# The opening of a Fourier mixing and SoLU kernel in another order of loads, products and conversions

## The chip, the cores and the metric

The kernel runs on one core of one Trainium2 chip. The metric is the device time of one execution in microseconds (us), taken as the median of several runs. The engines are named as in the profile: PE (TensorE), DVE (VectorE), ACT (ScalarE), POOL (GpSimd) and SP (SyncE, which here only issues DMAs).

## The reference

The input `x` has shape 8 x 3136 x 256. A two-dimensional Fourier transform is taken over its last two axes, and its real part is the input of a feed-forward block with a normalised activation.

```
X = fft(fft(x, axis=1), axis=2).real            # 8 x 3136 x 256
x = X.reshape(25088, 256)
h = x @ w_in                                    # 256 -> 1024
e = exp(h - max(h));  solu = h * e / (sum(e) + 1e-9)
ln = (solu - mean(solu)) / sqrt(var(solu) + 1e-6) * g_ln
out = ln @ w_out                                # 1024 -> 256
```

`x` and `g_ln` are float32. `w_in` and `w_out` arrive as float64, so that the kernel reads each number as two 32-bit words and makes a float32 of it itself.

## The kernel before, in words

The sequence axis of 3136 is split as 49 x 64. Two of the eight batches make a pair, and there are four pairs. A first transform over the 49 (`transform1`, on PE, with the table `F`) works on chunks of 4 of 32 positions; before it, `x` is folded: `add_mirror` adds the mirrored rows `xb` to the rows `xa`, and `fold` (for the first pair) adds and subtracts the two halves of the features, all on DVE. Eight chunks (`NC`) make one pair. The results `z` go to DRAM (`keep`), are read back in another layout (`turn`, into `g`), and a second transform over the 64 (`transform2`, table `T`) gives one block `q` for each of 25 frequencies. One such block is a unit (`Unit(p, k1)`), and there are 100 units.

A unit is multiplied by `Wi`, which is `w_in` already multiplied by the feature transform (`up`). `even` and `join` on DVE combine the two halves and take the row maxima, `expo` and `square` on ACT and `product` on DVE make the activation. The middle feature needs a rank-one term: `w_mid` times one column `r`, which `spread` brings from a row of `q` into the partitions by a small DMA. The activation is transposed and multiplied by `Wo` (`down`, or seven products of half size in `Down`), and each unit's result is stored. Units 0 to 4 (`whole = 4`) are transposed by PE (`turn_whole`); from unit 5 on a steady loop handles one unit while the down product runs five units behind (`lag = 5`) and the next pair's first transform is mixed in.

The order is written out by hand (`tc.manual_schedule()`): each engine runs its instructions in program order, and semaphores make them wait for their data. DMAs that SP issues go through one queue, those that POOL issues (the gathered loads of `xb`, parts of `turn`) through another.

The opening does the following before unit 0. `load_in`, `piece_in` read the four pieces of `w_in` (512 columns of 128 rows, 0.5 MB of float64 each). `exponent` takes the exponent field on DVE, `confine` clamps and shifts it in three ACT instructions (L529 to L531, or two DVE ones with `here=True`), and `narrow` builds the float32 number: two DVE instructions for the significand (L541, which the profile shows under the helper's line L507, and L543), one for the sign and exponent (L546), and one or two that multiply (L551). `product_in(h)` makes 128 rows of `Wi` (or `w_mid`, for `h = KD`) with four matmuls of 512 columns. `place_out`, `load_out`, `exponent_out` and `narrow_out` do the same for `w_out` in four pieces, scaled by `g_ln`. `centre` subtracts the mean over the 1024 rows from `Wo` (L631 to L633), and `weight_sums` makes the sums that the seven products need. Chunks 0 and 1 of `x` are loaded into buffers of `xpool`, chunks 2 to 5 into `rooms`, which are buffers of the transposed activation not yet in use, and chunks 6 and 7 into `xpool` again once chunks 0 and 1 are folded.

## Time and profile before

| | us |
|---|---|
| median of 3 runs (lowest, highest) | 1154.73 (1154.66, 1158.4) |
| the profiled execution, its own time | 1157.6 |
| its span in the profile | 1155.8 |
| PE busy | 1109.1 (96%) |
| DVE busy | 1013.8 (88%) |
| POOL busy | 848.0 (73%) |
| ACT busy | 758.3 (66%) |
| last instruction of the first transform of pair 0 (PE) ends | 48.8 |
| first unit's `even` starts | 59.6 |

The span runs from the first to the last instruction; the execution's own time has 1.8 us around it. Busy times of different engines overlap and don't add up. Line numbers such as L551 are those of the kernel before. A line of the timeline has start, length, engine, line, operation, the tile written and the tiles read, the number of instructions merged, and in brackets the idle time ahead of it with what ended it. The kernel is long against its opening: the first units start at about 5% of the span.

### The profile page before, as it was taken

To read this page: it belongs to the slowest core of one execution; us is meant where nothing else is said; L and a number is where in the kernel's file an instruction comes from. 1 tells how busy PE (TensorE), PEld (TensorE's weight loads), DVE (VectorE), ACT (ScalarE), POOL (GpSimd) and SP (SyncE) were. 2 spreads that over 40 slices of the span, in tenths; PEclk is the share of its full clock that TensorE was granted. 3 is DMA by queue.
4 is the path that set the end of the run, shared out by engine and by line. 5 is a ranking of instruction groups with operands and counts; after the bars stand their busy time and mean duration, and the time that the engine had idled before them with its cause. 6 is when DMAs were issued, how large, how long until landed. Compare 5 with 4: busy or idle time off the path is not lost.

```text
span 1155.8 us, 21664 instructions
## 1 busy us (share of the span) xinstructions
PE 1109.1 (96%) x7026; PEld 888.2 (77%) x7026; DVE 1013.8 (88%) x1440; ACT 758.3 (66%) x1725; POOL 848.0 (73%) x742
## 2 busy tenths in 40 slices
PE   2888999999999999999999999999999999999998
PEld 1555787888887778878887778878778788888887
DVE  7879988888999998888899998888898999898883
ACT  4567667666665766666666766666666676676661
POOL 3035888865898988866689888877499596777764
PEclk9999999999999999999999999999999999999999
DMA  9771798766998779866969697876697675865664
GB/s 238 204 192 39 168 191 195 184 145 145 160 187 160 180 177 184 198 138 143 164 139 204 150 189 171 203 175 141 149 159 146 137 163 122 150 144 111 139 135 111
DMA packets 458479, 185.75 MB, mean 161 GB/s; under 512 B 425750, under 2 KB 440350, under 8 KB 458368
## 3 DMA queue, kind: packets, MB, share of 16 engines
q1 hardware_dynamic: 444608, 146.22, 61.2%
q0 software_dynamic: 13760, 38.16, 12.4%
q8 instruction: 57, 0.93, 0.3%
q14 instruction: 54, 0.44, 0.1%
HBM read 44.78 MB, written 38.80 MB: 72 GB/s over the span
## 4 chain that ended last, share of the span: by engine, by line
PE 81%; DMA 5%; SPq 4%; DVE 4%; issue 2%; POOL 2%; ACT 1%; POOLq 0%; DVEq 0%; ACTq 0%
PE ps_m L401 48%; PE ps_h L264 25%; PE ps_m L208 4%; PE ps_m L236 3%; SPq L365 3%; DMA room<-in_x_dram 2%; DMA uT<-v 1%; DVE h L278 1%; POOL S L394 1%; DMA r<-q 1%; DVE u L293 1%; DMA F<-in_f_tab_dram 1%; SPq L216 1%; PE ps_m L468 1%; PE wps L601 1%
## 5 line engine op out<-in xcount | busy, mean ns | idle before, releaser
L264 PE MATMUL ps_h<-Wi,q 128*128 128x512 f32 x800 | 362.0, 594 | 7.9 <-DVE nmax L278 4.8
L394 POOL TENSOR_TENSOR S<-uT 128x512 f32<-128x512 f32 x186 | 251.1, 1350 | 104.6 <-DMA out_dram<-ot 40.9
L300 ACT ACTIVATE h<-u,usum 128x1024 f32<-128x1024 f32 x196 | 225.2, 1149 | 139.9 <-DVE u L293 139.9
L401 PE MATMUL ps_m<-Ws,S 128*128 128x128 f32 x2304 | 298.7, 276 | 4.3 <-issue 3.0
L401 PEld LDWEIGHTS ps_m<-Ws,S 128*128 128x128 f32 x2304 | 280.8, 192 | 8.8 <-issue 3.3
L264 PEld LDWEIGHTS ps_h<-Wi,q 128*128 128x128 f32 x800 | 144.0, 190 | 155.3 <-issue 139.9
L293 DVE SCALAR_TENSOR_TENSOR u<-h,u 128x1024 f32<-128x1024 f32 x196 | 259.4, 1359 | 0.8 <-ACT u L286 0.7
L286 ACT ACTIVATE u<-h,nmax 128x1024 f32<-128x1024 f32 x196 | 223.6, 1143 | 15.8 <-DVE nmax L278 11.8
L336 DVE STREAM_TRANSPOSE v<-u 128x2048 f32<-128x2048 f32 x93 | 215.5, 2317 | 3.2
L401 PE MATMUL ps_m<-Wo,uT 128*128 128x128 f32 x1536 | 213.1, 282 | 0.0
L401 PEld LDWEIGHTS ps_m<-Wo,uT 128*128 128x128 f32 x1536 | 197.3, 197 | 0.9 <-issue 0.9
L394 POOL TENSOR_TENSOR S<-uT,S 128x512 f32<-128x512 f32 x93 | 133.1, 1431 | 7.3
L278 DVE CUSTOM_DVE_ANT_0 h<-ev,ps_h 128x1024 f32<-128x1024 f32 x100 | 122.1, 1221 | 17.3 <-DVE ev L270 7.9
L479 POOL DMA_INDIRECT out_dram<-ot,idx x96 | 111.2, 1158 | 33.5 <-issue 16.6
L394 POOL TENSOR_TENSOR S<-S,uT 128x512 f32<-128x512 f32 x93 | 126.6, 1362 | 7.3
L278 DVE CUSTOM_DVE_ANT_0 h<-h,ps_h 128x1024 f32<-128x1024 f32 x96 | 117.3, 1221 | 14.2 <-ACT ot L444 0.5
L270 DVE SCALAR_TENSOR_TENSOR ev<-w_mid,r,ps_h 128x1024 f32<-128x1024 f32 x100 | 124.0, 1240 | 4.2 <-DMA r<-q 2.3
L401 PE MATMUL ps_m<-Ws,uT 128*128 128x128 f32 x768 | 106.2, 281 | 0.0
L401 PE MATMUL ps_m<-Wo,S 128*128 128x128 f32 x768 | 102.0, 276 | 0.7 <-ACT ot L435 0.7
L316 POOL TENSOR_TENSOR rs<-v,neg_half 128x2 f32<-128x2 f32 (+1 forms) x100 | 78.2, 782 | 28.4 <-ACT v L309 27.0
L236 PEld LDWEIGHTS ps_m<-T,g 128*128 128x128 f32 x400 | 60.1, 191 | 49.4 <-issue 45.8
L401 PEld LDWEIGHTS ps_m<-Ws,uT 128*128 128x128 f32 x768 | 98.0, 196 | 0.0
(96 smaller groups left out, 1135.5 us busy)
## 6 DMA issues: line engine op xcount, KB each, us to landing
uT<-v SPq DMA_DIRECT2D x752, 128.0 KB
out_dram<-ot SPq DMA_DIRECT2D x100, 128.0 KB
g<-zd POOLq DMA_DIRECT2D x72, 160.0 KB, 5.2
xa<-in_x_dram SPq DMA_DIRECT2D x28, 392.0 KB
zd<-z SPq DMA_DIRECT2D x24, 400.0 KB
raw_in<-in_moe_w_in_dram SPq DMA_DIRECT2D x4, 512.0 KB
raw_out<-in_moe_w_out_dram SPq DMA_DIRECT2D x2, 1024.0 KB
r<-q SPq DMA_DIRECT2D x100, 0.5 KB
```

Of the source, the lines that this page charges most:

```text
L236: nc.tensor.matmul(o, g[:, k, h * P : (h + 1) * P], table, start=(h == 0), stop=True, skip_group_check=True)
L264: nc.tensor.matmul(ps[:, fs], t.q[:, c * P : (c + 1) * P], Wi[:, c, fs], start=True, stop=True)
L270: nc.vector.scalar_tensor_tensor(out=t.ev, in0=w_mid, scalar=t.r, in1=ps, op0=ALU.mult, op1=ALU.add)
L278: nc.vector.tensor_tensor_reduce(out=t.h[s], in0=t.h[0] if s else t.ev, in1=t.odd, scale=1.0 if s else -0.5, scalar=3.0e38, op0=ALU.add, o ...
L286: nc.scalar.activation(out=t.u[s], in_=t.h[s], func=ACT.Exp, bias=t.nmax[:, s : s + 1], scale=-1.0, accum_out=t.esum[:, s : s + 1])
L293: t.last = nc.vector.scalar_tensor_tensor(out=t.u[s], in0=t.h[s], scalar=-1.0, in1=t.u[s], op0=ALU.mult, op1=ALU.mult, accum_out=t.usum[:, ...
L300: nc.scalar.activation(out=t.h[s], in_=t.u[s], func=ACT.Square, bias=t.usum[:, s : s + 1], scale=-float(FF), accum_out=t.ssq[:, s : s + 1])
L316: nc.gpsimd.tensor_tensor(out=t.rs[:, n], in0=t.v[:, n], in1=neg_half[:, n], op=ALU.pow)
L336: nc.vector.transpose(out=t.batch.v[:, t.w].rearrange("p f o -> p o f"), in_=t.both)
L394: i = engine.tensor_tensor(out=S[j], in0=a, in1=b, op=op)
L401: nc.tensor.matmul(o, a[:, c], b[:, c], start=start and c == 0, stop=c == n - 1, skip_group_check=True)
L479: dma = nc.gpsimd.indirect_dma_start(out=out, out_offset=bass.IndirectOffsetOnAxis(ap=idx[:, i : i + 1], axis=0), in_=t.ot[s], in_offset=None)
```

## The change

All loads of `x` for pair 0 are issued between the first and the second half of the columns of `w_in` (two pieces each). Chunks 6 and 7 get a room of their own, so that no load waits for a buffer. `product_in` works on half the columns at a time, and for the second half also on one row chunk at a time; its first halves stand between the first transforms. `g_ln` is loaded as 8 rows of 128 and transposed by PE. Chunk 5 is not folded by DVE: `transform1` reads its unfolded rows with four matmuls in place of two, with a negated table `minus`. `narrow` is split, so that the significand (`significand`) can be taken apart from the rest. `w_out` is loaded in two halves after the first transform, one ahead of `turn` and one behind the first `spread`, and its conversion is spread over the start of unit 0, unit 0 and unit 1. The second transforms of units 0 to 2, and three of the first four spreads (now on POOL's queue), are placed anew, and the constant columns `m` get a tile of their own.

```diff
--- before.py
+++ after.py
...
             pr.zs[c] = pr.z
-        y = pr.y[c]
         ps = result(0 if pr.p else s).rearrange("p (l d) -> p l d", l=2)
-        if s == NH // 2 - 1:
+        if c in pr.raw and not pr.p:
+            i, o = pr.raw[c][0][:, l : l + 2], ps[0:ZR]
+            up, down = slice(1, 128), slice(255, 128, -1)
+            for n, (cs, table, js) in enumerate(((EVEN, F[:, 0, :], slice(0, 129)), (up, F[:, 0, :], down),
+                                                 (ODD, F[:, 1, :], up), (ODD, minus, down))):
+                nc.tensor.matmul(o[..., cs], table, i[..., js], start=n == 0, stop=True, skip_group_check=True)
+            parts = []
+        elif s == NH // 2 - 1:
+            y = pr.y[c]
             parts = [(ps[0:ZR, 0], y[:, l], 0), (ps[0:ZR, 1], pr.y0[:, 0], 1), (ps[0:ZR, 1], y[:, l + 1], 2)]
         else:
-            parts = [(ps[0:ZR], y[:, l : l + 2], 0)]
+            parts = [(ps[0:ZR], pr.y[c][:, l : l + 2], 0)]
         pr.done.append(s)
...
 
-    def spread(t):
+    def spread(t, engine=nc.sync):
 
         t.r = small.tile([P, 1], FP32, tag="r", name="r")
-        nc.sync.dma_start(out=t.r, in_=t.q[0:1, P : 2 * P])
+        engine.dma_start(out=t.r, in_=t.q[0:1, P : 2 * P])
 
...
 
+    def significand(w, raw):
+
+        if w.dtype == FP32:
+            return
+        lo, hi = raw[:, 0 : 2 * NW : 2], raw[:, 1 : 2 * NW : 2]
+        bits(mantissa, hi, 0xFFFFF, ALU.bitwise_and, 0x100000, ALU.bitwise_or)
+        nc.vector.scalar_tensor_tensor(out=lo.bitcast(FP32), in0=lo.bitcast(U32), scalar=2.0 ** -32, in1=mantissa,
+                                       op0=ALU.mult, op1=ALU.add)
+
     def narrow(w, raw, outs, unit):
...
             return
-        lo, hi = raw[:, 0 : 2 * NW : 2], raw[:, 1 : 2 * NW : 2]
-
-        bits(mantissa, hi, 0xFFFFF, ALU.bitwise_and, 0x100000, ALU.bitwise_or)
-        m = lo.bitcast(FP32)
-        nc.vector.scalar_tensor_tensor(out=m, in0=lo.bitcast(U32), scalar=2.0 ** -32, in1=mantissa, op0=ALU.mult,
-                                       op1=ALU.add)
+        m, hi = raw[:, 0 : 2 * NW : 2].bitcast(FP32), raw[:, 1 : 2 * NW : 2]
 
...
             self.w_in = [fpool.tile([P, FF], FP32, tag="h", name="w_in", bufs=2) for _ in range(KD)]
-            self.pieces, self.units = [], []
-            for c in range(KD):
-                for j in range(0, FF, NW):
+            self.pieces, self.units, self.sums = [], [], {}
+            for j in range(0, FF, NW):
+                for c in range(KD):
                     i = 2 * (c * FF + j)
...
 
+        def significand_in(self, i):
+            significand(*self.pieces[i][:2])
+
         def narrow_in(self, i):
...
             nc.sync.dma_start(out=self.Q, in_=q_tab.rearrange("(c p) d -> p c d", p=P))
-            nc.sync.dma_start(out=g_ln, in_=moe_g_ln.rearrange("(c p) -> p c", p=P))
+            self.g8 = fpool.tile([P, D], FP32, tag="ot", name="g8", bufs=6)[0:KF, 0:P]
+            nc.sync.dma_start(out=self.g8, in_=moe_g_ln.rearrange("(c p) -> c p", p=P))
 
...
 
-            self.m = w_mid[:, 0 : KD * P].rearrange("p (c k) -> p c k", c=KD)
+            self.m = fpool.tile([P, D], FP32, tag="ot", name="m", bufs=6).rearrange("p (c k) -> p c k", c=KD)
             for c in range(KD):
...
 
-        def product_in(self, h):
-            ps = ps_h.tile([P, FF], FP32, tag=f"h{h % 2}", name="wps")
-            for half in range(2):
-                fs = slice(half * HW, (half + 1) * HW)
-                for c in range(KD):
-                    lhsT = self.m[:, c, :] if h == KD else self.Q[:, c, h * P : (h + 1) * P]
-                    nc.tensor.matmul(ps[:, fs], lhsT, self.w_in[c][:, fs], start=(c == 0), stop=(c == KD - 1))
-            nc.scalar.copy(w_mid if h == KD else Wi[:, h, :], ps)
+        def product_in(self, h, half, depth=range(KD)):
+            fs = slice(half * HW, (half + 1) * HW)
+            if depth[0] == 0:
+                if half and h == KD:
+                    self.sums[h] = result(3)[:, 0:HW]
+                else:
+                    self.sums[h] = ps_h.tile([P, FF], FP32, tag=f"h{h % 2}", name="wps")[:, fs]
+            for c in depth:
+                lhsT = self.m[:, c, :] if h == KD else self.Q[:, c, h * P : (h + 1) * P]
+                nc.tensor.matmul(self.sums[h], lhsT, self.w_in[c][:, fs], start=(c == 0), stop=(c == KD - 1))
+            if depth[-1] == KD - 1:
+                nc.scalar.copy(w_mid[:, fs] if h == KD else Wi[:, h, fs], self.sums[h])
 
...
         def scale_out(self):
-            nc.scalar.mul(out=g_ln, in_=g_ln, mul=2.0 ** -20)
+            ps = ps_h.tile([P, FF], FP32, tag="h1", name="g_ps")[:, 0:KF]
+            nc.tensor.matmul(ps, self.g8, ident[0:KF, 0:KF], is_transpose=True, start=True, stop=True)
+            nc.scalar.mul(out=g_ln, in_=ps, mul=2.0 ** -20)
 
...
             self.units.append(exponent(moe_w_out, self.raw[:, 2 * i * NW : 2 * (i + 1) * NW]))
+
+        def significand_out(self, i):
+            significand(moe_w_out, self.raw[:, 2 * i * NW : 2 * (i + 1) * NW])
 
...
             rooms[c], rooms[c + 1] = [room[:, i] for i in (0, 1)], [room[:, i] for i in (2, 3)]
+        room = fpool.tile([P, 2, FF, 2], FP32, tag="v", name="room_v", bufs=2)
         weights.load_in()
-        for c in range(4):
-            weights.piece_in(c)
-            if c:
-                load(first, c - 1, rooms.get(c - 1))
+        room = room[0:PR].rearrange("p a f b -> p (a f b)").rearrange("p (a n) -> p a n", a=4)
+        rooms[6], rooms[7] = [room[:, i] for i in (0, 1)], [room[:, i] for i in (2, 3)]
+        for i in range(2):
+            weights.piece_in(i)
+        for c in range(NC):
+            load(first, c, rooms.get(c))
+            if c == 0:
+                nc.sync.dma_start(out=F, in_=f_tab)
             if c == 1:
-                nc.sync.dma_start(out=F, in_=f_tab)
-        load(first, 3, rooms[3])
-        weights.load_tables()
-        for c in range(4, 6):
-            load(first, c, rooms[c])
+                weights.load_tables()
+        for i in range(2, 4):
+            weights.piece_in(i)
         nc.vector.memset(ones, 1.0)
...
             nc.vector.memset(t, 0.0)
-        weights.exponent_in(0)
-        weights.exponent_in(1)
+        weights.load_table(0)
+        for i in range(2):
+            weights.exponent_in(i)
+        for i in range(2):
+            weights.significand_in(i)
+            weights.narrow_in(i)
+        by_pe = (5,)
+        minus = fpool.tile([P, D], FP32, tag="ot", name="minus", bufs=6)[0:PR, 0:ZR]
+        nc.scalar.mul(out=minus, in_=F[:, 1, :], mul=-1.0)
         for c in range(NC):
-
-            if c == 0:
-                weights.narrow_in(0)
-                weights.narrow_in(1)
-            elif c < 3:
-                weights.narrow_in(c + 1)
-            if c < 2:
-                weights.exponent_in(c + 2)
             add_mirror(first, c, nc.vector)
-            fold(first, c)
-            if c == NC - 1:
-                for i in range(3):
-                    weights.exponent_out(i)
-            if c + 6 < NC:
-                load(first, c + 6)
-            if c == 3:
-                weights.place_out()
-                for i in range(2):
-                    weights.load_out(i)
-                weights.load_table(0)
-                weights.mid()
-                weights.scale_out()
+            if c not in by_pe:
+                fold(first, c)
             for s in range(CH // 2):
                 transform1(first, c * CH // 2 + s)
-            if c == 3:
-                weights.product_in(0)
-
+            if c == 0:
+                weights.mid()
+            if 1 <= c <= 1 + KD:
+                weights.product_in(c - 1, 0)
+        weights.place_out()
+        weights.load_out(0)
         turn(first, 0, nc.sync, 0, 2)
         turn(first, 0, nc.gpsimd, 2, KG)
-
-        confine(weights.units[0], True)
-        for i in range(1, 3):
-            confine(weights.units[i])
-        weights.product_in(1)
-        weights.narrow_out(0)
-        weights.exponent_out(3)
-        weights.product_in(2)
-        for i in range(1, 3):
-            weights.narrow_out(i)
+        for i in (2, 3):
+            weights.exponent_in(i)
+        weights.significand_in(2)
+        weights.narrow_in(2)
+        weights.significand_in(3)
+        weights.narrow_in(3)
+        weights.scale_out()
+        for i in range(2):
+            weights.exponent_out(i)
+        weights.significand_out(0)
 
         units = [Unit(p, k1) for p in range(NP) for k1 in range(NK)]
-        for t in units[:2]:
-            take2(t, transform2(pairs[0], t.k1))
-            spread(t)
-        confine(weights.units[-1])
-        for c in (2, 3, 0, 1, 4, 5, 6, 7):
-            keep(first, c, slice(4 * KG, ZR))
-        weights.load_table(1)
-        lag = 5
-        whole = 4
 
...
                 take2(t, transform2(pairs[t.p], t.k1))
-                spread(t)
+                spread(t, nc.gpsimd if 0 < i < 4 else nc.sync)
+
+        for h in (0, KD, 1):
+            weights.product_in(h, 1, range(1))
+        second_transform(0)
+        confine(weights.units[0])
+        weights.narrow_out(0)
+        for h in (0, KD, 1):
+            weights.product_in(h, 1, range(1, KD))
+        weights.load_out(1)
+        confine(weights.units[0])
+        lag = 5
+        whole = 4
 
...
         batches = []
-        begin(0)
+        enter(0)
+        even(units[0], up(units[0], 0))
+        weights.significand_out(1)
+        units[0].odd = up(units[0], 1)
+        second_transform(1)
+        second_transform(2)
+        for c in (2, 3, 0, 1, 4, 5, 6, 7):
+            keep(first, c, slice(4 * KG, ZR))
+        weights.load_table(1)
         for i in range(whole + 1):
...
             if i == 0:
-
-                weights.narrow_out(3)
+                weights.narrow_out(1)
+                for j in (2, 3):
+                    weights.exponent_out(j)
+                    confine(weights.units[-1])
+            if i == 1:
+                for j in (2, 3):
+                    weights.significand_out(j)
+                    weights.narrow_out(j)
             for s in cur.signs:
...
```

## The prediction

> **What bounds the kernel now.** I read the chain of waits first, because a change confined to the opening can only shift the time at which the steady part begins. Its columns are start, length and what ran.
>
> ```profile
> 11.17 24.83 DMA room<-in_x_dram
> 36.09 1.22 DVE room L134
> ...
> 46.45 2.39 PE ps_m L208 x16
> 48.84 6.88 PE wps L601 x16
> ...
> 69.61 8.23 DMA r<-q
> 77.95 1.29 DVE ev L270
> ...
> 113.84 1.11 PE ps_m L208 x4
> ```
>
> The opening is a relay. Until 36.1 us DMA sets the time (a chunk of x lands); then VectorE (DVE) folds four chunks without a pause, to 46.7; then TensorE (PE) runs the last first-stage transform and two weight products; then DVE processes units until about 113.8, after which the chain is PE almost alone. The table by windows, cut at these handovers, checks the relay. Columns: stretch and its length, then busy time (and instructions) of PE, PE weight loads, DVE, ACT and POOL, granted clock, DMA share, GB/s.
>
> ```profile
> 36.00:46.70 10.70, 9.39 (x34) 5.32 (x33) 10.51 (x24) 5.01 (x8) 0.00 (x0) 1.00 0.96 323
> 46.70:59.60 12.90, 11.97 (x45) 6.77 (x44) 10.08 (x22) 9.19 (x14) 2.48 (x4) 1.00 0.29 82
> 59.60:77.95 18.35, 16.37 (x72) 10.59 (x70) 14.55 (x21) 11.52 (x25) 5.76 (x5) 1.00 0.96 238
> 77.95:113.80 35.85, 28.35 (x122) 17.16 (x122) 34.10 (x48) 26.41 (x57) 18.23 (x20) 1.00 0.21 51
> ```
>
> DVE is full from 36.0 to 46.7 and again from 77.95 on (34.10 of 35.85). Between them it is idle 2.8 + 3.8 = 6.6 us. From 120 us PE is busy 10 of every 10 us. So whatever moves the DVE line of unit 2's `even` (77.95) moves the whole run, one for one. The timeline at that place gives the waits in brackets:
>
> ```profile
> 59.62 1.28 DVE L270 SCALAR_TENSOR_TENSOR ev<-w_mid,r,ps_h 128x1024 f32<-128x1024 f32 x1 [1.92 <-ACT S L530]
> 73.34 2.29 DVE L633 TENSOR_TENSOR Wo<-Wo,wbar 128x2048 f32<-128x2048 f32 x1 [0.43 <-ACT wbar L632]
> 77.95 1.28 DVE L270 SCALAR_TENSOR_TENSOR ev<-w_mid,r,ps_h 128x1024 f32<-128x1024 f32 x1 [2.31 <-DMA r<-q]
> ```
>
> The first is unit 0's `even`; the last waited for r of unit 2, issued by SP at 69.6, behind eight `keep`s and a table in the same queue.
>
> **What the Trainium skill says.** "DMA: Bandwidth & Descriptors", section "Why a DMA increments its semaphore by 16 and not by 1": a copy is spread over the largest count up to 16 that divides its rows, so x's 98 rows get 14 engines and the weights' 128 rows 16. The trace fits: 369 GB/s at 4 to 6 us (w_in alone), 219 to 231 at 22 to 26 (mostly x). No view shows single engines. The same page, "Queues, rings and completion order": an engine takes turns between its queues. The trace agrees: SP's queue and POOL's each hold 48 to 54% at 10 to 20 us. "TensorE: Matmul & The Clock Gate", section "What's actually happening": PE runs at half clock after about 3.4 us of idling. The trace agrees, though its clock row shows 1.00 throughout: eight records of L208 take 3.73 us at 18.3 and 1.89 at 39.4.
>
> **The change, part by part.**
>
> *Loads.* Up to 8 us SP's queue carries the same things in the same order (idx, two w_in pieces, x, F). Then before's SP queue still had w_in pieces 2 and 3 (1.05 MB) and g_ln's 1024 packets of 4 B among the x. These packets are visible: 674 packets moved only 0.38 MB at 30 to 32 us. Now from 8 us SP moves xa1 to xa7, Q and x0 (3.2 MB), and POOL all eight xb (3.2 MB) without the two waits for a free buffer (5.9 and 6.5 us in the timeline). POOL's indirect loads of before landed 3.2 to 3.5 us apart (first at 14.0, sixth at 30.7); two more at 3.3 put the eighth at 37.3. SP's half at the same 0.12 MB/us takes about 26.5 us, 34.5, and lands by 37 too. I take 37.3 (35.6 to 39). DVE needs 2.65 us per chunk, so it has no backlog, and the last chunk takes 2.8 (43.88 to 46.68): x is folded at **40.2** instead of 46.7, 6.5 us earlier. Chunk 5 folded by PE removes 1.55 us of DVE (0.69 + 0.68 + 0.17) where DVE waits for data anyway: nothing. The extra matmuls and the halves of the products (two of 0.86 us per half) lie in PE's own wait for x: nothing.
>
> *DVE work moved behind x.* Conversions of w_in pieces 2 and 3 stood under the loading; now they follow it: 2 x (0.43 + 0.42 + 0.69 + 0.75 + 0.69) = 5.95 us. The two-step clamp on DVE (`confine(..., True)`, 0.88) goes to ACT. Net **+5.1 us**.
>
> *Waits of DVE behind x.* These I placed instruction by instruction:
> - z of chunk 7 is copied 2.8 us after the fold (as before, 49.47 against 46.68): 43.0. Only then can ACT clamp piece 2 (three of 0.72, 2.2 in all): 45.2. DVE is ready for it at 42.2: idle 3.0.
> - DVE narrows piece 2 (46.6), then piece 3 (49.1), takes two exponents and one significand of w_out: 51.0.
> - PE has the three column products of row chunk 0 from 46.7, 3 x 0.86: 49.3. The turned g: the keep takes 1.95 us, the turn 3.7 as before, and its SP half now stands behind `load_out(0)` (1 MB at the 390 GB/s of 40 to 44 us, 2.7), which started earlier: about 49.1. Second transform of unit 0, then q at 50.3.
> - ACT clamps w_out piece 0 (52.5), then copies the three half products at 0.58: Wi 53.1, w_mid 53.7, Wi 54.3. DVE narrows the piece (1.58) to 54.1, idle 1.5.
> - PE's `up` of unit 0 takes 1.98 after 53.1; `even` starts at 55.2, idle 1.1. That is **4.4 us earlier** than 59.62.
>
> From there DVE still owes what before had mostly behind it: the rest of w_out, 1.07 + 1.58 + 0.88 + 2 x 2.65 = 8.8 us against 3.1. In order: even 55.2 to 56.6, significand 57.8 (with the wait for `up`), join 59.1, narrow 60.7, two exponents 61.6, product 62.75, even and two joins of unit 1 to 66.8, pieces 2 and 3 to 72.1, two products 74.4, wbar 74.9 (0.5 idle, behind ACT's square as before), Wo 77.25. ACT's two further clamps end at 65.5, before DVE uses them. Unit 2's `even` at **77.3**; r of unit 2 no longer delays it, because POOL issues that spread before the keeps' bulk. The books agree: fold 6.5 earlier, 5.1 of work added, and 7.4 idle up to unit 2 where it was 6.6.
>
> *Clock of PE.* PE idles from about 42.4 to 46.7. If that makes the three products run cold, they end at 51.0, q at 52.1, `even` of unit 0 at 57.0, unit 2's at 79.0. I give this 2 in 5 for want of a way to see its window, which weighs +0.7 in the middle; the r2 wait gone is counted above. Bounds of this term: 0 to +1.7.
>
> *Queues.* SP: `load_out(1)` waits behind the spread of unit 0 (52) and is landed near 58, wanted at 60.7. The z_u keeps follow it and land near 59, when unit 0's `expo` wants that buffer. Keeps (2.6 MB at 280 GB/s, 9.4 us) and T end near 69, turn 1 near 74, wanted at about 84. POOL: the spreads of units 1 to 3 stand behind the turn (ended at 48) and before power and pair 1's loads, none of which anyone waits for until 95. A spread from POOL is not in the trace: it cannot land before its issue, so at best it hides; the nearest row, POOL's turns, lands in 2.5 to 6.0 us; SP's r of unit 2 took 8.2. Taken: 4, hence r1 at 62.3, just in time for 62.8; 0 to +3.7. g_ln's transpose is one small matmul and one 0.2 us ACT copy beside DVE's conversions: nothing. Centring and `weight_sums` move with Wo by 1.6 us (75.6 to 77.25) and are first used after 100.
>
> **Sum.** 77.5 (77.3 with a part of the clock term) against 77.95: -0.45 us. The profiled execution took 1157.6 around a span of 1155.8, 2.9 above the median of 1154.73; the difference is applied to the median: **1154.3 us**. 0.5% (5.8 us) is about what a measurement of this kernel can tell from no change.
>
> **Rivals.**
> - *The waits close up* (chance 0.15). If x lands at 35.6 (-1.7) and the three idles of DVE before unit 0 (5.6 us) mostly vanish, because g or the clamps come sooner, 1148 to 1149. For it: DMA is full throughout the loading, so 1.05 MB less is real. Against: ACT's order (z copies, clamp, clamp) is fixed.
> - *A transfer takes the place of the removed waits* (0.17). r of unit 1 now shares the engines with 1 MB of w_out and the keeps. If it lands 8.2 us after issue, as r of unit 2 did, `even` of unit 1 starts at 66.5 instead of 62.8: +3.7 - 0.45, 1158; with cold products too, 1160. It decides from a landing at 63.3 on.
> - *x comes late* (0.08). All x together on 14 engines may go below 219 GB/s; folded after 40.7 the change loses, at 47 it passes 0.5%: 1157 to 1161.
> - The forecast itself has 0.60, with its own range 1151.5 to 1157.5.
>
> **Range and chances.** The tails of the rivals reach 1150 and 1160: about 2 in 10 lie outside. Faster by over 0.5% 0.12 (most of the first rival), slower by over 0.5% 0.15 (parts of the other two, in combination), within 0.73.
>
> **What would show it.** Right: last DVE fold near 40, two DVE waits for ACT clamps near 42 to 45 and 51 to 52.5, unit 0's `even` near 55, Wo minus wbar near 75 to 77, PE in its steady rhythm near 113 to 114. Wrong: L633 before 72 or after 80; an `ev` row with a wait for r over 2 us; a fold of the last chunk after 42 or before 38; DVE idle under 3 us between the fold and unit 0.

## The result and the profile after

The change makes the kernel slower. Its median is 1165.98 us (1164.38 to 1167.79, 4 runs) against 1155.93 us (1154.66 to 1158.4, 4 runs) for the kernel before: a ratio of 1.0085, interval 1.006 to 1.011. The forecast was 1154.3, with a range that ended at 1160. The profiled execution took 1164.38 us, with a span of 1162.5; the kernel before had 1157.6 and 1155.8, so the two traces differ by 6.7 us. The profiled execution of after was the fastest of its four, which is one reason why the medians stand further apart than the traces; what the traces explain below is 6.5 us, not 10.

The chain of waits of the kernel after, in the same columns (start, length, what ran). Lines of the code have moved: L215 and L204 are `transform1`, L619 `product_in`, L538 the last step of a clamp, L557 and L562 the end of `narrow`, L243 and L249 the second transform and its copy, L277 `even`, L271 `up`, L657 Wo minus wbar.

```profile
23.38 1.22 DVE room L134
...
40.19 3.92 PE ps_m L215 x24
44.13 0.59 ACT z_g L218
44.74 1.78 DMA zd<-z_g
...
61.62 7.22 DMA r<-q
68.93 1.29 DVE ev L277
...
79.97 4.69 PE ps_h L271 x8
...
120.31 1.11 PE ps_m L215 x4
```

Loading sets the time up to 23.4 us now, not 36.1. But the steady part begins at 120.31 instead of 113.84, and the longest step on the way there is r of unit 1, which took 7.22 us to arrive.

The table by windows, cut at the last fold (41.08) and at `even` of units 0 and 2, in the columns of before:

```profile
41.08:58.85 17.77, 12.95 (x42) 6.81 (x41) 9.04 (x20) 11.54 (x20) 2.55 (x4) 0.90 0.55 139
58.85:83.17 24.32, 16.80 (x53) 9.61 (x52) 20.28 (x32) 13.82 (x26) 4.36 (x6) 0.86 0.86 251
83.17:120.30 37.13, 31.68 (x146) 19.89 (x144) 34.24 (x49) 28.66 (x63) 20.47 (x21) 1.00 0.07 15
```

DVE is the third busy column: 9.04 of 17.77 us, then 20.28 of 24.32. Its idle time between the fold and unit 2's `even` is 8.73 + 4.04 = 12.77 us, where before had 6.6. The work in that stretch is 29.32 us against 10.11 + 14.55 = 24.66 before: 4.66 more, close to the 5.1 of the forecast. With a fold that ends 5.6 us earlier (41.08 for 46.68) the books close: 4.66 + 6.2 - 5.6 = 5.2, which is 83.17 - 77.95. A further 1.2 us is lost after it (37.13 against 35.89 to the steady part).

The timeline of DVE in the kernel after names the waits:

```profile
46.88 0.75 DVE L557 SCALAR_TENSOR_TENSOR S<-raw_in,top_bit,S 128x512 int32<-128x512 int32 x1 [3.98 <-ACT S L538]
...
56.28 0.75 DVE L557 SCALAR_TENSOR_TENSOR S<-raw_out,top_bit,S 128x512 int32<-128x512 int32 x1 [3.12 <-ACT S L538]
...
58.85 1.28 DVE L277 SCALAR_TENSOR_TENSOR ev<-w_mid,r,ps_h 128x1024 f32<-128x1024 f32 x1 [0.90 <-ACT S L536]
...
68.93 1.28 DVE L277 SCALAR_TENSOR_TENSOR ev<-w_mid,r,ps_h 128x1024 f32<-128x1024 f32 x1 [3.05 <-DMA r<-q]
...
80.97 2.29 DVE L657 TENSOR_TENSOR Wo<-Wo,wbar 128x2048 f32<-128x2048 f32 x1 [0.43 <-ACT wbar L656]
83.17 1.27 DVE L277 SCALAR_TENSOR_TENSOR ev<-w_mid,r,ps_h 128x1024 f32<-128x1024 f32 x1
```

The first wait is for a clamp behind the copies of z, which end at 44.72; the second names a clamp too, but that clamp stood on ACT behind the copy of q, and q behind PE. The fourth is r of unit 1. Unit 2's `even` (last line) waits for nothing: the 2.31 us that before lost there are gone, as forecast.

The timeline of PE in the kernel after shows why q was late:

```profile
48.41 2.07 PE L619 MATMUL wps<-w_in,Q 128*128 128x512 f32 x2 [4.16 <-DVE w_in L562]
50.28 1.71 PE L619 MATMUL ps_m<-w_in,m 128*128 128x512 f32 x2
51.83 1.02 PE L619 MATMUL wps<-w_in,Q 128*128 128x512 f32 x2
53.02 0.68 PE L243 MATMUL ps_m<-T,g 128*128 128x128 f32 x4 [0.18 <-DMA g<-zd]
```

After 4.16 us without work, the first products take about twice what the third takes (1.87 us from the first line's start to the second's, 0.86 being the rate of a warm pair), so that the three run from 48.41 to 52.85, 4.4 us instead of 2.6. The turned g arrives at the same moment, 53.0, so that this view alone can't tell which of the two delays q.

PE was slow at two other places. In the chain of waits every step from 26.22 to 44.13 is PE's, and the table by windows of after, cut where its granted clock (the third number from the end) changes, shows it at half where a transform and the first half product stood, between z and q, and at unit 2's `up`:

```profile
24.35:27.76 3.41, 1.54 (x7) 1.24 (x8) 2.05 (x6) 0.98 (x2) 0.00 (x0) 1.00 0.98 227
27.76:31.17 3.41, 3.41 (x6) 1.62 (x5) 2.89 (x6) 0.75 (x2) 0.00 (x0) 0.50 0.91 216
...
44.83:48.24 3.41, 0.00 (x0) 0.00 (x0) 1.33 (x2) 3.29 (x5) 0.91 (x2) 1.00 0.65 130
48.24:51.65 3.41, 3.24 (x4) 1.50 (x5) 2.82 (x6) 0.79 (x2) 1.64 (x3) 0.50 1.09 342
...
68.72:72.13 3.41, 1.84 (x8) 1.44 (x8) 2.91 (x4) 3.38 (x9) 1.36 (x3) 1.00 0.73 208
72.13:75.54 3.41, 0.44 (x2) 0.28 (x2) 3.34 (x8) 2.03 (x4) 1.81 (x2) 1.00 1.07 210
75.54:78.95 3.41, 2.59 (x7) 1.50 (x7) 3.34 (x7) 0.00 (x0) 0.00 (x0) 0.50 0.96 255
78.95:82.36 3.41, 3.41 (x7) 1.68 (x6) 2.98 (x5) 1.51 (x3) 0.00 (x0) 0.50 0.44 130
```

The clock changes at 27.76, 31.18, 48.24, 51.66, 75.54 and 82.38 us. The distances are 1, 5, 1, 7 and 2 times 3.41 us. Ahead of the three falls PE was busy for 1.54, 0.00 and 0.44 of 3.41 us, ahead of the three returns for 3.41, 3.24 and 3.41. After 1.84 (68.72 to 72.13) it did not fall, and after 2.59 (75.54 to 78.95) it did not return.

### The profile page after: what moved, and what is told of

It reads as the page before. It is cut to its first block, busy times and chain, and to the rows that moved or that the text cites. A ratio compares the mean times of both kernels' runs of the same rounds, so it can differ in the third digit from the quotient of the medians.

```text
span 1162.5 us, 21680 instructions
## 1 busy us (share of the span) xinstructions
PE 1113.4 (96%) x7035; PEld 890.6 (77%) x7035; DVE 1011.7 (87%) x1435; ACT 761.3 (65%) x1732; POOL 854.7 (74%) x745
## 3 DMA queue, kind: packets, MB, share of 16 engines
q0 software_dynamic: 13856, 38.16, 12.2%
## 4 chain that ended last, share of the span: by engine, by line
PE 83%; DMA 4%; DVE 4%; issue 3%; SPq 3%; POOL 2%; ACT 1%; POOLq 0%; DVEq 0%; ACTq 0%
PE ps_m L408 48%; PE ps_h L271 26%; PE ps_m L215 5%; PE ps_m L243 3%; SPq L372 3%; DMA room<-in_x_dram 2%; DMA uT<-v 1%; DVE h L285 1%; DVE u L300 1%; DMA r<-q 1%; PE ps_m L475 1%; POOL S L401 1%; ACT h L307 0%; DVE ev L277 0%; PE wps L619 0%
## 5 line engine op out<-in xcount | busy, mean ns | idle before, releaser
L271 PE MATMUL ps_h<-Wi,q 128*128 128x512 f32 x800 | 363.1, 595 | 6.0 <-DVE nmax L285 4.4
L271 PEld LDWEIGHTS ps_h<-Wi,q 128*128 128x128 f32 x800 | 144.6, 191 | 154.6 <-issue 141.2
L277 DVE SCALAR_TENSOR_TENSOR ev<-w_mid,r,ps_h 128x1024 f32<-128x1024 f32 x100 | 124.0, 1240 | 4.0 <-DMA r<-q 3.1
L243 PEld LDWEIGHTS ps_m<-T,g 128*128 128x128 f32 x400 | 60.1, 191 | 49.4 <-issue 46.4
L408 PEld LDWEIGHTS ps_m<-Wo,S 128*128 128x128 f32 x768 | 94.2, 193 | 0.8 <-issue 0.8
```

The lines of the kernel that those rows point to most:

```text
L243: nc.tensor.matmul(o, g[:, k, h * P : (h + 1) * P], table, start=(h == 0), stop=True, skip_group_check=True)
L271: nc.tensor.matmul(ps[:, fs], t.q[:, c * P : (c + 1) * P], Wi[:, c, fs], start=True, stop=True)
L277: nc.vector.scalar_tensor_tensor(out=t.ev, in0=w_mid, scalar=t.r, in1=ps, op0=ALU.mult, op1=ALU.add)
L408: nc.tensor.matmul(o, a[:, c], b[:, c], start=start and c == 0, stop=c == n - 1, skip_group_check=True)
```

## The experiments

All start from the kernel after unless said otherwise. "Steady" is the start of pair 1's first transform on PE, where everything before it has been paid. Three groups were run, each beside the kernel before; its medians there were 1158.18 (e1 to e4), 1157.50 (e5 to e8) and 1157.51 us (e9 to e12). The kernel after is not in these groups, so that ratios and not medians are compared with it. Since the traces of one kernel differ in the opening too, the variants of the change are best compared stretch by stretch (us, from the timelines; fold is the end of the last fold, z the end of the last copy of z, u0 to u2 the `even` of units 0 to 2; the clock is the granted one from 24 to 32 us):

| | clock | fold | z | z to u0 | u0 to u1 | u1 to u2 | u2 to steady | steady |
|---|---|---|---|---|---|---|---|---|
| before | 1.00 | 46.68 | 49.47 | 10.15 | 6.59 | 11.74 | 35.89 | 113.84 |
| after | 0.79 | 41.08 | 44.72 | 14.13 | 10.08 | 14.24 | 37.14 | 120.31 |
| e1, chunk 5 on DVE | 0.79 | 41.65 | 44.44 | 13.75 | 10.97 | 14.34 | 36.73 | 120.23 |
| e2, w_out in the gap | 0.81 | 40.55 | 45.76 | 13.78 | 11.49 | 14.24 | 36.67 | 121.94 |
| e3, e2 and PE warm | 1.00 | 39.85 | 42.68 | 12.72 | 10.85 | 14.25 | 37.00 | 117.50 |
| e4, keeps late | 1.00 | 41.40 | 44.26 | 14.49 | 12.24 | 14.25 | 36.52 | 121.76 |
| e10, PE warm | 1.00 | 40.31 | 43.10 | 13.83 | 11.10 | 14.25 | 36.53 | 118.81 |
| e9, r by SP | 1.00 | 40.11 | 43.21 | 14.67 | 6.80 | 15.60 | 35.91 | 116.19 |
| e5, e3 and r by SP | 1.00 | 40.10 | 42.96 | 12.70 | 6.80 | 15.60 | 35.90 | 113.96 |

Among the variants of the change only e1 alters the work that stands ahead of z, so that the columns fold and z show how one code varies. Two things move z. One is the fold, which ended between 39.85 and 41.65: z comes 2.8 to 2.9 us after it in before, e1, e3, e4, e5 and e10, and 3.1 in e9. The other is PE at half clock, which made it 3.6 in after and 5.2 in e2, but not in e1, where the fold was late as well. (The row of granted clocks does not show PE's slow start: in before it reads 1.00, though eight records at 25.36 took 3.73 us.)

**e1: chunk 5 folded by DVE again.**

```diff
-        by_pe = (5,)
+        by_pe = ()
```

> The changed kernel with chunk 5 folded by DVE again. In the changed kernel the chain of waits runs through PE from 26 to 44 us, and the four-matmul form of chunk 5 takes 4.1 us there against 1.9. Theory A (PE bound the end of loading because of this edit): z of chunk 7 is copied at about 43.2 instead of 44.7 and the run is 1.5 us shorter. Theory B (DVE is as late as PE): DVE folds chunk 5 in 1.55 us, of which only 1.0 is idle, so its last fold ends 0.6 us later at 41.7, PE ends its last transform 2.4 us after that, at 44.1 as now, and the time does not change.

Measured: 1165.76 us, ratio 1.0061 (1.0037 to 1.0086), unit 0's `even` at 58.19, steady 120.23. At the same clock as after z came 0.3 us sooner and nothing was left of it at the end. The fold ended 0.6 us later (41.65), PE waited 0.39 us for it ahead of its last transform, and z followed 2.8 us after the fold: theory B. In these two traces the chunk on PE costs and brings nothing.

**e2: w_out loaded in the gap of the loads.**

```diff
-        weights.place_out()
-        weights.load_out(0)
         turn(first, 0, nc.sync, 0, 2)
...
                 weights.product_in(c - 1, 0)
+            if c == 4:
+                weights.place_out()
+                weights.load_out(0)
```

> The changed kernel with the first half of w_out issued after chunk 4's transform instead of ahead of the turn (DMA stands nearly idle from 41 to 46 us). Theory A (w_out ahead of it in SP's queue made g late): g lands 5.6 to 6 us after z is copied, at 50.5 instead of 53.0, and unit 0's even moves from 58.9 to about 56.5. Theory B (the three products on a cold PE end at 52.85 in any case): g lands early, but the second transform of unit 0 still starts at 53.0, and even and the whole run do not move. Both: the 0.5 us wait of DVE for w_out at 51.3 goes.

Measured: 1164.33 us, 1.0058 (1.0041 to 1.0075). The wait for raw_out went and g was there in time, but the products still took 4.4 us (49.45 to 53.80); `even` of unit 0 at 59.54, steady 121.94. Freeing g alone brings nothing.

**e3: the same, with PE kept busy.** Four matmuls that nobody reads, ahead of the second half of the products.

```diff
+        weights.warm(4)
         for h in (0, KD, 1):
             weights.product_in(h, 1, range(1))
```

> As e2_wout_in_gap, and four more matmuls of 512 columns, whose result nobody reads, fill PE's idle time between the last first-stage transform and the products of the second half of w_in. Theory A (clock): the three products take 2.6 us instead of 4.4 and end at 51.0, q of unit 0 is copied at 52.1 instead of 54.1, even of unit 0 starts at 57.0, 1.9 us earlier than in the changed kernel, and the run is 1.9 us shorter than e2. Theory B (not the clock but the operands make them slow): the products still take 4.4 us and nothing moves against e2.

Measured: 1164.01 us, 1.0051 (1.0028 to 1.0075). The timeline of PE in e3:

```profile
46.48 1.10 PE L619 MATMUL wps<-w_in,Q 128*128 128x512 f32 x2 [0.64 <-DVE w_in L562]
...
48.27 1.02 PE L619 MATMUL wps<-w_in,Q 128*128 128x512 f32 x2
49.58 0.68 PE L243 MATMUL ps_m<-T,g 128*128 128x128 f32 x4 [0.29 <-DMA g<-zd]
```

The same six records now take 2.6 us, and unit 0's `even` starts at 55.40, where the prediction had put it (55.2). Of the 3.45 us against after, 2.0 come from z (1.2 of them from a fold that ended sooner, 0.8 because PE was not behind), and 1.4 from the stretch that was edited (12.72 for 14.13). The wait for r of unit 1 remained (3.78 us).

**e10: the warm matmuls alone**, with w_out back ahead of the turn.

> The kernel after with four matmuls of 512 columns that no one reads put ahead of the second half of the products, and nothing else: w_out stays ahead of the turn. Theory A (two things have to go together for unit 0: the products must be warm and g must not stand behind w_out): products take 2.6 us from 46.9, but the second transform of unit 0 still waits for g until 52.8 to 53, so unit 0's even stays at 57.8 to 58.9 and the steady start at 119 to 120.5. Rival B (the clock alone was the delay): even of unit 0 at 55 to 56.5, steady start 117 to 118.

Measured: 1165.74 us, 1.008 (1.0054 to 1.0106), the ratio of after. The products took 2.6 us, but the second transform then waited 1.39 us for g (to 51.11), and the stretch from z to unit 0 is 13.83, level with after. (`even` of unit 0 at 56.93 and steady at 118.81 lie a little below theory A's bands because z came 1.6 us sooner.) The four traces without an edit in this stretch (after, e1, e4, e9) have 13.75 to 14.67, e2 and e10 with one edit 13.78 and 13.83, e3 and e5 with both 12.72 and 12.70. So the cold products and the late g lie side by side, either alone holds up unit 0, and only both edits together bring 1 us or more.

**e4: keeps behind `even` of unit 1** (six keeps and T moved in the order of the program).

```diff
+            if i == 0:
+                for c in (0, 1, 4, 5, 6, 7):
+                    keep(first, c, slice(4 * KG, ZR))
+                weights.load_table(1)
```

> The changed kernel with only the keeps of chunks 2 and 3 where they were; the other six and the second part of the T table are issued after unit 1 has begun. Theory A (r of unit 1 was held up by the keeps' traffic): r of unit 1 lands 3 to 4 us after its issue instead of 7.2, DVE's 3.05 us wait at 65.9 goes, and the run is 3 us shorter. Theory B (it is the route through POOL's queue that is slow): r still lands 7 us after its issue, and the run does not move. Theory C (the traffic is only moved): r of unit 1 is early, but r of unit 2 or 3, or the second turn, becomes late and takes 1 to 3 us back.

Measured: 1166.4 us, 1.0083 (1.0058 to 1.0108), wait for r 5.34 us, steady 121.76. A miss by construction: nothing on SP waits between the old place and the new one, so SP issued the keeps at the same time, 55.7 to 62.7. To delay a DMA one must put it behind an instruction that waits. Whether the keeps' traffic or the route through POOL's queue delays r therefore stays open here.

**e5: e3 with r by SP**, ahead of six of the keeps.

```diff
-                spread(t, nc.gpsimd if 0 < i < 4 else nc.sync)
+                spread(t)
...
-        second_transform(1)
-        second_transform(2)
-        for c in (2, 3, 0, 1, 4, 5, 6, 7):
+        for c in (2, 3):
+            keep(first, c, slice(4 * KG, ZR))
+        second_transform(1)
+        second_transform(2)
+        for c in (0, 1, 4, 5, 6, 7):
             keep(first, c, slice(4 * KG, ZR))
```

> As e3_wout_and_warm, but r of units 1 to 3 is issued by SP, behind the second half of w_out and the keeps of chunks 2 and 3 and ahead of the other six keeps. Theory A (r of unit 1 is late because its 128 small packets in POOL's queue share the engines with megabytes of keeps in SP's): in SP's queue it stands ahead of 1.9 MB of keeps and lands 2 to 4 us after its issue instead of 7 to 8; DVE's wait of 3.8 us ahead of even of unit 1 goes, and the run is 3 to 3.5 us shorter than e3. Theory B (whatever is behind r, a busy set of DMA engines delays it): the wait stays at 3 us or more, or r of unit 2 takes its place.

Measured: 1159.16 us, 1.002 (1.0011 to 1.0028). `even` of unit 1 at 62.46 without a wait, steady 113.96, level with the 113.84 of before. Of the 6.35 us against after, 1.76 come from z, 1.43 from PE and g, 3.16 from r (-3.28, +1.36 and -1.24 in the last three stretches).

**e9: r by SP alone** (the edit shown for e5), PE cold and w_out where the change put it.

> The kernel after with one thing changed: r of units 1 to 3 is issued by SP behind the keeps of chunks 2 and 3 and ahead of the other six; TensorE is left cold and w_out where it is. Theory A (r's landing and the cold clock add up, each on its own): unit 0's even stays at 58.2 to 59.6, the wait for r at unit 1 (3.05 us) goes, unit 1's even at 65.7 to 67, unit 2's at 80 to 81, steady start 117 to 118.5, ratio to before 1.004 to 1.007. Rival B (with the chain before unit 0 late, r is no longer what unit 1 waits for; product or the clamps are): unit 1's even moves by under 1 us, steady start 119.5 to 121.

Measured: 1160.68 us, 1.0032 (1.0019 to 1.0044), steady 116.19, 4.1 us below after, of which 1.5 is z; without that it would be 117.7, in theory A's band. The timeline of DVE in e9:

```profile
64.68 1.28 DVE L277 SCALAR_TENSOR_TENSOR ev<-w_mid,r,ps_h 128x1024 f32<-128x1024 f32 x1
68.83 1.22 DVE L285 CUSTOM_DVE_ANT_0 h<-h,ps_h 128x1024 f32<-128x1024 f32 x1 [1.50 <-ACT h L307]
...
80.28 1.27 DVE L277 SCALAR_TENSOR_TENSOR ev<-w_mid,r,ps_h 128x1024 f32<-128x1024 f32 x1
```

From unit 0 to unit 1 it is 6.80 us instead of 10.08. Unit 1's `even` (first line) waits for nothing. The edit changes two things about r, its queue and what moves beside it: six keeps now stand behind it, and the share of the DMA engines is 0.19 from 61 to 62 us and 0.04 from 62 to 63, where after has 1.03 and 1.04. The wait for ACT in the second line takes back part of it between units 1 and 2. The gain after unit 2 (35.91 for 37.14) is a second effect of r: while DVE waits for it, PE has no work, and in after it then runs the eight records of unit 2's `up` in 4.90 us at a clock of 0.50. In e9 they take 3.60, and the window is

```profile
76.00:80.00 4.00, 4.00 (x15) 2.09 (x14) 3.57 (x5) 1.51 (x3) 0.00 (x0) 1.00 1.05 223
```

The variants of the change divide in the same way: 36.5 to 37.1 us after unit 2 in the six that wait for r at unit 1 (after, e1 to e4, e10), 35.9 in the four that don't (e5, e6, e9, e11).

**e8: the kernel before, with the conversion of w_out's pieces 1 and 2 behind unit 0's joins.**

```diff
         weights.product_in(2)
-        for i in range(1, 3):
-            weights.narrow_out(i)
...
             if i == 0:
-                weights.narrow_out(3)
+                for j in range(1, 4):
+                    weights.narrow_out(j)
```

> The kernel before with one part of the change: the narrowing of w_out pieces 1 and 2 is moved from before unit 0's even to behind its join, so that pieces 1 to 3 stand there. Theory A (DVE work moved across unit 0's even is paid in full, because PE sets the start of even and DVE all that follows): even of unit 0 stays at 59.6, Wo minus wbar is 5.3 us later at 78.6, and since the 2.3 us wait for r of unit 2 goes with it, unit 2's even and the run are 3.0 us later. Theory B (DVE has other slack there): the run moves by less than 1 us.

Measured: 1161.88 us, 1.0044 (1.003 to 1.0058). The timeline of DVE in e8:

```profile
60.85 1.28 DVE L270 SCALAR_TENSOR_TENSOR ev<-w_mid,r,ps_h 128x1024 f32<-128x1024 f32 x1 [7.11 <-ACT S L530]
72.73 1.28 DVE L270 SCALAR_TENSOR_TENSOR ev<-w_mid,r,ps_h 128x1024 f32<-128x1024 f32 x1
82.50 1.27 DVE L270 SCALAR_TENSOR_TENSOR ev<-w_mid,r,ps_h 128x1024 f32<-128x1024 f32 x1
```

Taking 5.3 us of work out of the stretch before unit 0 only made DVE wait 7.11 us there: the fold of this run ended about 1.2 us late, and `even` of unit 0 came 1.2 us late. PE's products and q set that stretch, not DVE, so the conversion had been free there. Behind `even` it costs in full: 21.65 us from unit 0 to unit 2 against 18.33, that is 5.6 more less the 2.3 of the old wait for r.

**e6: an attempt, e5 with all of w_out loaded early and its significands in DVE's waits.**

```diff
+            if c == 5:
+                weights.load_out(1)
...
-        weights.significand_in(2)
-        weights.narrow_in(2)
-        weights.significand_in(3)
-        weights.narrow_in(3)
+        for i in (2, 3):
+            weights.significand_in(i)
+        weights.significand_out(0)
+        weights.narrow_in(2)
+        weights.narrow_in(3)
```

> As e5_r_by_sp, and all of w_out is loaded in the gap behind x; the significands of all four pieces and the first piece's narrowing are done by DVE before unit 0's even, in its waits for ACT and for q. Theory A (what the change lost is that it gave DVE the w_out conversion behind unit 0 while DVE idled 8.7 us before it): 3.6 us less work behind unit 0's even, even itself not later (54 to 55.5), Wo minus wbar 3 to 4 us earlier than in e5, the run about 3.5 us shorter than e5 and level with the kernel before or up to 4 us faster. Theory B (the waits before unit 0 are a chain ACT - DVE - PE, and more DVE work in it only delays even): even moves 3 us or more and nothing is gained against e5.

Measured: 1159.56 us, 1.0019 (1.001 to 1.0029), steady 116.23. A wait for raw_out of 2.49 us came first, then PE waited 2.47 us for g and went cold again; `even` of unit 0 at 60.80. The added work lay on the chain to unit 0.

**e11: a second attempt, e5 with DVE's waits for ACT removed.**

```diff
         weights.significand_in(2)
+        confine(weights.units[0], True)
         weights.narrow_in(2)
...
-        second_transform(0)
         confine(weights.units[0])
         weights.narrow_out(0)
         for h in (0, KD, 1):
             weights.product_in(h, 1, range(1, KD))
+        second_transform(0)
```

> An attempt at a faster version. The kernel after with warm products, w_out loaded in the gap and r by SP (the three edits tried before), and then: the clamp of piece 2 of w_in is done by DVE itself (0.88 us, where it waited 3.21 us for ACT), the clamp of w_out's first piece stands on ACT ahead of q of unit 0, all six products ahead of the second transform of unit 0, and the significand of w_out's second piece ahead of unit 0's even. Theory A (what is left there are waits of DVE for ACT's order): piece 3 ready at about 46.8 (48.97 without these), unit 0's even at 53.3 to 54.5, unit 2's at 75 to 76, steady start 110.5 to 112, that is 2 to 3 us below the kernel before in the profile, ratio 0.997 to 1.0. Rival B (g's arrival near 49.6 and the up products behind it bind): unit 0's even not before 55, steady start 113 to 114, ratio 1.000 to 1.003.

Measured: 1160.55 us, 1.003 (1.0012 to 1.0047), steady 115.68. The timeline of DVE in e11:

```profile
55.09 1.28 DVE L277 SCALAR_TENSOR_TENSOR ev<-w_mid,r,ps_h 128x1024 f32<-128x1024 f32 x1 [2.54 <-ACT S L538]
...
62.95 1.23 DVE L300 SCALAR_TENSOR_TENSOR u<-h,u 128x1024 f32<-128x1024 f32 x1 [2.23 <-ACT u L293]
```

The narrowing of w_out began 3.3 us sooner than in e5 (49.82 for 53.09), and DVE then waited 2.54 us ahead of `even`, since all six products stood ahead of the second transform on PE (which ended at 52.5), and 2.23 us for unit 0's `expo` on ACT. Waits were traded for waits. Unit 0's `even` and the ratio are as rival B had them, the steady start (113 to 114) is not.

**e12: the kernel before, with unit 2's second transform and spread beside those of units 0 and 1.**

```diff
-        for t in units[:2]:
+        for t in units[:3]:
             take2(t, transform2(pairs[0], t.k1))
...
-            second_transform(i + 2)
+            if i:
+                second_transform(i + 2)
```

> The kernel before with one thing taken over from the change: the second transform and the spread of unit 2 stand ahead of the keeps, beside those of units 0 and 1, still on SP. Theory A (r of unit 2 stood behind the keeps): the wait of 2.31 us at unit 2's even goes, even at 75.6 to 76.2, steady start 111.5 to 112, ratio 0.997 to 0.999. Rival B (another wait is next, ps or q copy on ACT, or the extra q copy delays unit 0): unit 2's even moves by under 1 us, ratio 0.999 to 1.001.

Measured: 1157.36 us, 0.9997 (0.9987 to 1.0008). The timeline of DVE in e12:

```profile
61.85 1.28 DVE L270 SCALAR_TENSOR_TENSOR ev<-w_mid,r,ps_h 128x1024 f32<-128x1024 f32 x1 [3.72 <-ACT S L530]
```

The wait of 2.31 us at unit 2 is gone, yet unit 2 starts only 0.16 us sooner (77.79), since `even` of unit 0 is 2.2 us later (61.85 for 59.62). Of these, 1.1 come from a fold that ended late in this trace (47.74 for 46.68) and 1.2 from the edit (z to unit 0 takes 11.32 us for 10.15): one more second transform and its copy stand ahead of unit 0's `up` on PE (the third starts at 59.33). Without the late fold the trace would be about 1.2 us ahead of before; the medians differ by 0.15 us, and the interval reaches to 1.5.

**e7: the kernel before, with g_ln in rows.**

```diff
-            nc.sync.dma_start(out=g_ln, in_=moe_g_ln.rearrange("(c p) -> p c", p=P))
+            nc.sync.dma_start(out=self.g8, in_=moe_g_ln.rearrange("(c p) -> c p", p=P))
...
-            nc.scalar.mul(out=g_ln, in_=g_ln, mul=2.0 ** -20)
+            nc.tensor.matmul(ps, self.g8, ident[0:KF, 0:KF], is_transpose=True, start=True, stop=True)
+            nc.scalar.mul(out=g_ln, in_=ps, mul=2.0 ** -20)
```

> The kernel before with one part of the change: g_ln loaded as 8 rows of 128 and transposed by PE. Theory A (g_ln's 1024 packets of 4 bytes blocked SP's queue for about 5 us from 28 to 33 us): chunk 4 is usable at about 32 to 33 instead of 36.1 us, the last fold ends 3 to 3.5 us earlier, and the run is about 3 us shorter, since PE follows at once. Theory B (the engines are busy with the other queue's bytes anyway): chunk 4 moves by 1.5 us, and the run by 1 or less.

Measured: 1159.7 us, 1.0012 (0.9997 to 1.0027), no difference that a measurement tells. Neither theory fits its trace. The data came sooner at chunk 4, but a piece of w_in was late among the x (a wait of DVE of 3.76 us at 17.01), and later a fold waited 3.63 us, to 47.74, for PE to free a buffer, with PE slow up to 41 us (eight records of L208 in 3.7 us); `even` of unit 0 came at 64.75. Why PE was slow there this run doesn't tell.

## Why the prediction was wrong

Three terms of the forecast failed. The largest is r of unit 1, which was taken to land after 4 us and took 7.2. The cold products were given 0.2 us in the sum and cost 1.8. And PE, which was said to wait for x, had no margin left when its clock fell. The steps side by side (us):

| step | forecast | measured |
|---|---|---|
| last fold of x ends | 40.2 | 41.08 |
| z of chunk 7 copied | 43.0 | 44.72 |
| clamp of w_in's piece 2 ready | 45.2 | 46.84 |
| three products of row chunk 0 | 46.7 to 49.3 | 48.41 to 52.85 |
| g | 49.1 | 53.0 |
| `even` of unit 0 | 55.2 | 58.85 |
| r of unit 1, issue to landing | 4 | 7.2 |
| `even` of unit 1 | 62.8 | 68.93 |
| Wo minus wbar | 74.9 | 80.97 |
| `even` of unit 2 | 77.3 | 83.17 |
| steady (113.84 - 0.45) | 113.4 | 120.31 |

**What held.** The fold came 5.6 us earlier (6.5 forecast), the work moved behind it was 4.66 us (5.1), the chunk folded by PE was neutral in e1's trace, the wait for r of unit 2 went, and from unit 1 to unit 2 it took 14.24 us (14.5). The work moved behind `even` cost in full, which e8 shows on the kernel before. One reading of the forecast was generous: 14 of 16 engines would bring 369 GB/s down to 323, while the trace had 219 to 231, so that the number of engines alone does not explain the rate of x.

**The step that put the extra matmuls and half products "in PE's own wait for x: nothing" failed**, since it left PE no margin, and with it "z of chunk 7 is copied 2.8 us after the fold" failed in after. At full clock the step held: 2.8 to 2.9 us in e3, e4, e5 and e10, 3.1 in e9. In after two steps from 26.22 stood at half clock (a transform of eight records and a half product of four took 2.21 + 3.15 us, in e9 1.94 + 1.72), and PE could not make up for the 1.70: from there to 44.13 the chain is PE's without a gap, 9.00 of 9.00 us busy from 32 to 41. z came at 44.72 for 43.0. Of these 1.7 us, 0.8 are PE (3.64 us after the fold for 2.8). The other 0.9 are the fold, 41.08 for 40.2: DVE waited for the data of chunk 6 until 35.67 and then folded chunks 6 and 7 without a pause. e4 shows this second part by itself, with a clock of 1.00, a fold at 41.40 and z at 44.26.

**The term "Clock of PE", 0 to +1.7 at 2 in 5, measured +1.8, and the step "g at 49.1" was 3.9 late beside it.** The forecast's own idle stretch was 4.3 us (42.4 to 46.7), and "TensorE: Matmul & The Clock Gate", section "What's actually happening", gives about 3.4 us of idling for the half clock: the term should have been taken in full. The forecast also wrote that it weighs 0.7 in the middle, and put only 0.2 into its sum. The trace of after shows 4.16 us idle, a granted clock of 0.50 from 48.24 to 51.65, and 4.4 us for 2.6 us of products. Behind w_out g came at 53.0 in after and 51.1 in e10, without w_out ahead of it at 49.6 in e3. 1.7 for z and 1.9 from z to unit 0 (14.13 for 12.2) make up the 3.65 us at unit 0; e3 and e5, with warm products and an early g, get 1.4 of the 1.9 back.

The same section says that the monitoring window runs free, so that slow stretches fall differently in each run of one kernel. The traces agree, and they show the window: in all eleven whose clock changes in the opening (after, e1 to e6 and e8 to e11) the changes stand whole multiples of 3.41 us apart, with an offset of their own in each; in after the fall at 1160.98 us, the last, is still 332 such steps from the first. Where the page asks for an idle window, the measurement goes further, and it decides: half of one is enough. All 22 falls up to 120 us follow a window in which PE was busy for at most 0.50 of it, and no window with a share under 0.50 went without one (PE's slow start aside, which the rows don't show). The returns follow shares of 0.86 and more; up to 0.84 the clock stayed down. So luck decides about a short pause: 1.93 us of idling from 24.29 to 26.22 lie within one window in after (24.35 to 27.76), while the 1.89 us from 24.01 to 25.90 in e9 are cut by a border at 24.76, and e9 kept its clock. A pause of 4.16 us leaves some window more than half idle wherever it falls; all five traces that have it (after, e1, e2, e4, e9) ran the products cold.

**The term "Taken: 4" for a spread from POOL was 7.2**, and this is the largest part of the loss: the rival "A transfer takes the place of the removed waits", with a place (unit 1) that was right and a price (+3.7) that was near, held at 0.17. The wait was 3.05 us, and 1.2 more followed from PE going cold meanwhile, which no step had. Taking the wait away gives 3.2 us back in the traces (e5 against after), and e9, which does that alone, has a ratio of 1.0032 where after has 1.0085. The queues of after from 61.6 to 65.0 us (packets, MB, share of 16 engines; then a row of the issues with its KB and the us to landing):

```profile
q1 hardware_dynamic: 391, 1.34, 102.2%
...
r<-q POOLq DMA_DIRECT2D x2, 0.5 KB, 7.5
```

SP's queue moves keeps and the table; POOL's, with two spreads issued, moves not a packet in these 3.4 us. "DMA: Bandwidth & Descriptors", section "Queues, rings and completion order", has an engine taking turns between its queues, and the opening of before agrees with it (49 to 57% each from 10 to 20 us; the forecast read 48 to 54). That a tiny transfer on POOL's queue was not served at once beside a full SP queue contradicts this only if its packets were already there. Whether they were not yet made or made and not served isn't shown. Nor is it shown that POOL's queue is the cause: e5 and e9 take r away from that queue and from the keeps' traffic at once, e4 did not part the two, and in before r of unit 2 took 8.23 us on SP's queue behind the keeps.

**The chances.** Cold products, a late g and a late r were put into separate cases, "with cold products too, 1160" as the far end. They happened together. The cold products and the late g overlap, but what they cost adds to z's delay and to that of r: 3.65 up to unit 0, 2.5 to unit 1 (10.08 for 7.6), -0.3 to unit 2, 1.2 after it, less the 0.2 of the clock term that the sum already held, make 6.9, which is 120.31 - 113.4.

**What stays open.** The medians of after and before are 10 us apart where the traces show 6.7, and e5 measures 1.002 where its trace is level with before. Executions of one kernel differ by up to 8 us (1153.28 to 1161.65 for before in one group), and each trace is one execution; that e5's had the early z (1.76 us) would fit its 0.2%. Four of the ten traces of the change and its variants have the slow stretch while loading (after, e1, e2, e6), which is too few for its share of all executions. No version tried beats the kernel before; e12 equals it.

## What to carry to other kernels

When loads are moved ahead of the work that filled an engine's wait, ask what every engine does meanwhile: a PE without slack passes a fall of its clock on, one that idles for 4 us pays on its next products, and a small load can wait for microseconds while a bulk one moves, even though it has another queue. Work that stood beside a longer chain was free there and costs its whole length when it is moved behind it. Mishaps that don't exclude each other belong in one sum of the forecast, not in cases side by side.

## What the runs showed of the hardware that was not expected

- A spread of 0.5 KB by POOL landed 7.2 and 7.8 us after its issue in after, beside SP's full queue, the first with no packet for 3.4 us; spreads by SP, placed ahead of the bulk, kept nobody waiting (e5, e9).
- The granted clock of PE changes only at whole multiples of 3.41 us from one another, with an offset that differs from run to run (eleven traces, up to 120 us). It fell after each window in which PE was busy for less than half, and came back after a window with a busy share of 0.86 or more. A pause of 1.93 us was enough in after.
- A fall costs at least one whole window: in after the clock was at half for 3.41, 3.41 and 6.84 us, the last because PE was busy for only 2.59 us of the first 3.41.
